# A linear-attention and two-layer float32 kernel: one elementwise line from GpSimd to ScalarE, the weight conversions' products from GpSimd to VectorE, and new instruction orders inside a step

## The chip, the cores and the metric

The kernel runs on one core of a Trainium2 chip. The metric is the device time of one execution in microseconds (us). Three executions of the kernel before took 1710.34, 1711.36 and 1712.08 us; the median is 1711.36 us. Engines are named as the profile names them: PE is TensorE's matmuls and PEld its weight loads, DVE is VectorE, ACT is ScalarE, POOL is GpSimd, SP is SyncE, which here issues the transfers.

## The reference, cut to what matters

Everything is computed to float32 precision. The weights of both layers arrive as float64; q, k and v are float32.

```python
# 8 batches, 8 heads, 576 positions, 64 per head -> x: 4608 tokens x 512
kv  = einsum('bhsd,bhse->bhde', k, v)   # k^T v per head
out = q @ kv;  x = out / sqrt(mean(out*out) + 1e-6) * g_norm
# first layer, d_ff = 2048
h = x @ w_in
P = a[0] + a[1]*h + a[2]*h*h + a[3]*h*h*h
Q = 1.0 + abs(b[0])*abs(h) + abs(b[1])*h*h
x2 = (P / (Q + 1e-6)) @ w_out
# second layer, d_ff = 1024
out = (((x2 @ w1) * (x2 @ w2)) @ w3) @ w_out2
```

## The kernel before, in words

**Number format.** A float32 operand is split into a rounded part `hi` (made by a ScalarE copy) and a rest `lo` (a VectorE or GpSimd subtraction); a product is three matmuls, hi·hi, hi·lo and lo·hi (`mm3`, L87 to L90). A float64 weight tile is turned into float32 by `to_f32` (L144): two ScalarE instructions make the sign (L149, L150), three VectorE instructions move the exponent and mantissa over (L152, L156, L160), and one product of both gives the float32 tile (L164, on GpSimd).

**Steps.** The first layer runs in 192 steps. A step g is one block of 384 tokens (12 blocks) times one slice of 128 of d_ff (16 slices). In step g TensorE computes h for that slice (`l1`, 12 matmuls of 384 columns) and then multiplies the finished activation of step g - 3 with `w_out` (`l2`, 12 matmuls). Between the two lies the elementwise work, spread over three steps:

- `ew1(g)`, in step g: ScalarE makes a = |h| (L512) and the innermost line n of the numerator P (L513). The inner line of Q, s = |b1|·a + |b0|, is L514 on GpSimd, and L517 multiplies it with a, also on GpSimd. VectorE brings the numerator further (L520, L522; both read h in PSUM).
- `ew2(g - 1)`: ScalarE makes an approximate reciprocal from s (L530, L531), VectorE improves it by a Newton step and multiplies with the numerator (L533, L535, L537). All three read two tiles of SBUF.
- `ew3(g - 2)`: ScalarE's `hi` (L502) and VectorE's `lo` (L504) of the result, which `l2` of the next step needs.

**What sets the order.** The program is scheduled by hand: each engine runs its instructions in the order in which the Python code writes them. Within a step, these pieces are generators that stop (`yield`) between VectorE instructions, and `mix` advances them by the letters of a string: n is ew1, s is ew2, l is ew3, and t, u, v are weight conversions. `MIX[0]` holds for the first 23 steps, `MIX[1]` for the others. ScalarE's and GpSimd's order follows from the same strings, since a piece's first part (up to its first `yield`) writes their instructions.

**Weight conversions.** 32 tiles of 128x512 are needed by the first layer itself: 11 are converted before step 0 and 21 in steps 0 to 22 (`CONV`). Each is also split: ScalarE copies `hi` (L84), GpSimd subtracts (L85), since `w_next` passes `nc.gpsimd` to it. 80 half tiles of 128x256 of the second layer's weights are converted from step 32 on, in 9 of 16 steps (`bg_conv`), and go back to DRAM as float32. In the last block (from step 176) the second layer's tiles are loaded again and split (`slot_split`, L625): 16 on GpSimd, 8 on VectorE.

**Attention.** The next blocks' x (36 tiles of 128 tokens) is computed between the matmuls of the steps, with small matmuls (L266, L318, L331, L373) and a few instructions each on ScalarE and VectorE. The second layer follows the steps and is TensorE's alone, apart from evictions.

Of the kernel before, what the change touches and what calls it, by code (L numbers as in the profile page):

```python
# [12 lines left out]
AF = mybir.ActivationFunctionType  # L13
# [5 lines left out]
def linear_attention_two_moe_kernel(  # L19
# [15 lines left out]
):  # L35
    """x = rmsnorm(q (k^T v)) per head; g = P(x w_in) / Q(x w_in); x2 = g w_out;
    out = ((x2 w1) * (x2 w2)) (w3 w_out2).

    The float64 weights come as their bits and become float32 on the chip (within float32's range;
    what is below it becomes 0). Float32 operands are split exactly into hi + lo float32r parts (12 + 12 bits), and a product  # L40
    is hi hi + hi lo + lo hi, accumulated in float32. Activations stay feature-major, so that the
    weights are the stationary operands as they lie in DRAM.
    """
    nc = tc.nc
# [46 lines left out]

    # ---- weights in SBUF: slot s of wa holds a [P, KD, P] slice, slot s of wb a [P, DM] row tile,
    # first as float64 bits, then as float32r hi and lo
    wa, wb = {}, {}
# [42 lines left out]
    def mix(order, **gens):  # L137
        """The generators' VectorE instructions in this order, so that none waits for the one before."""
        for c in order:
            next(gens[c], None)  # L140
        for gen in gens.values():
            run(gen)

    def to_f32(raw, t, n=W):  # L144
        """float64 bits to float32: exponent and mantissa moved over, times the sign (0 for 0 and
        for what is below float32's range). The low words' place takes the magnitude."""
        hw, lw = raw[:, :, 1], raw[:, :, 0]
        ti = t.bitcast(I32)
        nc.scalar.activation(out=ti, in_=f32(hw), func=AF.Copy, scale=0.47 * 2.0**15)  # L149
        nc.scalar.activation(out=t, in_=ti, func=AF.Sign)  # L150
        yield
        nc.vector.tensor_scalar(  # L152
            out=lw, in0=lw.bitcast(U32), scalar1=2.0**-29, scalar2=7.0, op0=ALU.mult, op1=ALU.min
        )
        yield
        nc.vector.scalar_tensor_tensor(  # L156
            out=lw, in0=hw, scalar=3, in1=lw, op0=ALU.logical_shift_left, op1=ALU.bitwise_or
        )
        yield
        nc.vector.tensor_scalar(  # L160
            out=lw, in0=lw, scalar1=0x7FFFFFFF, scalar2=0x40000000,
            op0=ALU.bitwise_and, op1=ALU.bitwise_xor,
        )
        nc.gpsimd.tensor_tensor(out=t, in0=f32(lw), in1=t, op=ALU.mult)  # L164

# [6 lines left out]
    def conv_on(depth=DEPTH):  # L172
        """The next stage of every conversion but the last depth."""
        for p in pend[:max(0, len(pend) - depth)]:
            p[1].pop(0)(p[0])
            if not p[1]:
                pend.remove(p)
# [5 lines left out]
    def conv(raw, *stages):  # L183
        """A tile's conversion; its later stages follow the starts of the next ones."""
        t = f32_tile(W)
        yield from to_f32(raw, t)
        pend.append((t, list(stages)))
        conv_on()
# [6 lines left out]

    # ---- constants
    ident = const.tile([P, P], F32, name="ident")
# [19 lines left out]

    # ---- attention
    atp_cm = tc.tile_pool(name="atp", bufs=1)
# [4 lines left out]
    def segs(i):  # L224
        """Row ranges of token tile i: (first row, rows, batch, position in the sequence)."""
        r, left = [], P
        t = i * P
        while left:
            b, s = divmod(t, S)
            n = min(left, S - s)  # L230
            r.append((P - left, n, b, s))
            t += n
            left -= n
        return r
# [20 lines left out]
    def kv_part(i, c):  # L255
        """Part c of tile i's k^T v, two heads to a product (a tile has rows of two batches at most)."""
        sg = segs(i) if i < NTILE else []
        if c >= len(sg):
            return
        kk = kt[i].rearrange("p h d -> p (h d)")  # L260
        vv = vt[i].rearrange("p h d -> p (h d)")
        r0, n, b, s = sg[c]
        if s == 0:
            kvps[0] = ps_tile("kv", [P, NP, P])
        for p in range(NP):
            nc.tensor.matmul(  # L266
                kvps[0][:, p, :],
                lhsT=kk[r0:r0 + n, p * P:(p + 1) * P],
                rhs=vv[r0:r0 + n, p * P:(p + 1) * P],
                start=(s == 0 and p == 0),  # L270
                stop=(s + n == S),
                skip_group_check=True,
            )
        if c == len(sg) - 1:
            del kt[i], vt[i]

    def kv_out(i):
        """The diagonal blocks of a batch's k^T v to SBUF, where tile i holds the batch's last row."""
        for r0, n, b, s in segs(i) if i < NTILE else []:
            if s + n == S:  # L280
                dst = kvbd[b % 2]
                nc.scalar.copy(dst[0:D, :, 0:D], kvps[0][0:D, :, 0:D])
                nc.vector.tensor_copy(dst[D:P, :, D:P], kvps[0][D:P, :, D:P])
# [10 lines left out]
    def at_tile(shape, i, name):  # L294
        """The first block's tiles have their own room, the others share one."""
        if i < T0:
            return p0[0].tile(shape, F32, tag=name, name=name)
        return atp.tile(shape, F32, tag="at", name=name)

    def at_ps(i, name):  # L300
        """The first block's tiles also have a PSUM bank each."""
        if i < T0:
            tag = {"q": ("acc0", "acc1", "acc2", "acc3"), "o": ("h", "h", "at", "acc0"), "x": ("acc1", "acc2", "acc3", "at")}[name][i]
        else:
            tag = "at"
        return ps_tile(tag, [P, NP, P], 2 if tag == "h" else 1)
# [53 lines left out]
    def n_out(i):  # L360
        """The tile times -2 / rms, by one Newton step."""
        po, ms, y, y2 = at[i]
        nc.vector.tensor_tensor(out=y2, in0=ms, in1=y2, op=ALU.mult)
        nc.vector.scalar_tensor_tensor(out=y, in0=y2, scalar=3.0, in1=y, op0=ALU.subtract, op1=ALU.mult)
        x = at_tile([P, H, D], i, "xt")
        nc.vector.tensor_tensor(out=x, in0=po, in1=y.unsqueeze(2).to_broadcast([P, H, D]), op=ALU.mult)
        at[i] = x
# [19 lines left out]
    with tc.manual_schedule():  # L387
        p0_cm = tc.tile_pool(name="p0", bufs=T0)
        p0[0] = p0_cm.__enter__()
        NKV0 = -(-S // P)  # L390
        # The steps (block, part of d_ff): the first two blocks share the first half of the weights
        # before the second half is there
        HM = MF // 2
# [17 lines left out]
        def w_next():  # L411
            kind, i = w_seq[n_cv[0]]
            n_cv[0] += 1
            return (conv_a if kind == "a" else conv_b)(i, nc.gpsimd)

# [3 lines left out]

        # What comes before the steps: loads (W weights, K k and v, Q q), C conversions, F their last stages,  # L420
        # and per token tile k k^T v, t q's transpose, o its product and squares, r rms, n normed, x split
        count = {}
# [60 lines left out]
        def x2_out(j, m):  # L483
            """The block's x2 to DRAM; the first block's comes in two parts."""
            for n in range(KD):
# [20 lines left out]
        def ew1(g):  # L506
# [6 lines left out]
            nc.scalar.activation(out=n, in_=h, func=AF.Identity, scale=na[:, 3:4], bias=na[:, 2:3])  # L513
            nc.gpsimd.tensor_scalar(  # L514
                out=s, in0=a, scalar1=ab[:, 1:2], scalar2=ab[:, 0:1], op0=ALU.mult, op1=ALU.add
            )
            nc.gpsimd.tensor_tensor(out=s, in0=s, in1=a, op=ALU.mult)  # L517
# [25 lines left out]

        # The next blocks' attention: what is done in step g at the places 0 (its start), 1 (behind the first
        # products), 2 (before the split), 3 (before the end), 4 (its end)
        todo = {}
# [40 lines left out]

        # ---- the second part's weights as float32 to DRAM, half a tile at a time
        HW = W // 2
# [26 lines left out]

        # ---- second part: out = ((x2 w1) * (x2 w2)) W
        def slot_load(kind, s, src):
# [74 lines left out]

        # ---- W = w3 w_out2: its rows take the second half of wb, w_out2 the first
        w3t = {}
# [32 lines left out]
        def w_step(i):  # L728
            """W's row i, with row i + 1's transposes; row i - 1 to SBUF."""
            if i == 0:  # L730
# [7 lines left out]

        MIX = "ttssntslntltsn", "sssnnllnnstttt"
        CONV = "11101101120111111111111"  # L740
        NG = NBA * MF
        LB = NG - MF
        for g in range(NG + SK):
            if g >= LB:
                if g > LB:
# [3 lines left out]
                    if 2 <= s and s - 2 < MF:  # L749
                        slot_split(("a", s - 2), nc.gpsimd)  # L750
                s = g - LB - SK - 1
# [92 lines left out]
```

## Time and profile before

| | us |
|---|---|
| median of three executions | 1711.36 |
| span of the profiled execution | 1712.4 |
| TensorE busy | 1615.6 (94%) |
| VectorE busy | 1134.9 (66%) |
| ScalarE busy | 831.2 (49%) |
| GpSimd busy | 612.2 (36%) |

The profile gives the span of the execution that it shows (first to last instruction), 1712.4 us, and no separate device time of that execution; the span is 1.0 us above the median of the runs. The shares of busy time mix parts of the program with different limits: before step 0, the 192 steps, and the second layer. The rows below are therefore taken from stretches of the span. Step g starts where ScalarE's L512 of that step starts: step 0 at 60.2 us, step 23 at 212.7, step 176 at 975.8, step 191 at 1045.5. Neighbouring instructions of an engine overlap a little in the trace, so what one costs its engine is the distance from its start to the next one's start.

### The profile page before, as it was taken

The numbers are of one execution on the slowest core, as the hardware profiler recorded it, in microseconds if no ns is written. First come the engines' busy times: TensorE is split into PE (matmuls) and PEld (weight loads), VectorE is DVE, ScalarE is ACT, GpSimd is POOL, SyncE is SP. The second block draws the span as 40 slices with busy tenths as digits, with TensorE's granted clock in tenths as the row PEclk, the third lists the DMA queues.
The fourth block names the chain that finished last, engine by engine and source line by source line (L and its number), as shares of the span: only waits on it lengthen the run. The fifth ranks groups of instructions, "written<-read, shape, count | busy, mean of one in ns | idle before, by whom it ended". The sixth has DMA issues, their size and how long they took to land.

```text
span 1712.4 us, 22970 instructions
## 1 busy us (share of the span) xinstructions
PE 1615.6 (94%) x8384; PEld 1450.9 (85%) x8384; DVE 1134.9 (66%) x1949; ACT 831.2 (49%) x1701; POOL 612.2 (36%) x552
## 2 busy tenths in 40 slices
PE   4777799999999999999999999999999999999999
PEld 3676799999999999999999888788888888888887
DVE  5999989999999999999999997222222222222221
ACT  4667666666666667676666675211112112111211
POOL 5689944545555555454545585000000000000000
PEclk9899999999999999999999999999999999999999
DMA  9634113333332332342212142301001001010000
GB/s 238 161 94 128 31 44 93 78 81 87 93 94 70 94 84 77 81 103 71 71 50 66 44 151 71 111 0 50 25 25 49 25 25 44 7 49 25 25 25 25
DMA packets 175154, 118.43 MB, mean 69 GB/s; under 512 B 118720, under 2 KB 152512, under 8 KB 175040
## 3 DMA queue, kind: packets, MB, share of 16 engines
q1 hardware_dynamic: 175040, 116.95, 24.7%
q8 instruction: 66, 1.08, 0.3%
q14 instruction: 48, 0.39, 0.1%
HBM read 86.77 MB, written 30.15 MB: 68 GB/s over the span
## 4 chain that ended last, share of the span: by engine, by line
PE 47%; DVE 32%; issue 7%; ACT 7%; POOL 5%; DMA 2%; SPq 1%; DVEq 0%; POOLq 0%; ACTq 0%
PE h L88 6%; PE h L90 6%; PE h L89 6%; PE acc L89 5%; PE acc L88 5%; PE acc L90 5%; DVE s L537 4%; DVE n L520 4%; DVE s L533 4%; DVE n L522 4%; DVE lo L504 4%; DVE s L535 3%; POOL s L517 2%; PE at L89 2%; PE kv L89 2%
## 5 line engine op out<-in xcount | busy, mean ns | idle before, releaser
L514 POOL TENSOR_SCALAR s<-a,ab 128x384 f32<-128x384 f32 x192 | 190.8, 994 | 198.1 <-ACT a L512 184.5
L517 POOL TENSOR_TENSOR s<-s,a 128x384 f32<-128x384 f32 x192 | 228.1, 1188 | 16.0
L530 ACT ACTIVATE y<-s,epsq 128x384 f32<-128x384 f32 x192 | 117.7, 613 | 160.7 <-POOL s L517 160.2
L535 DVE SCALAR_TENSOR_TENSOR s<-s,y 128x384 f32<-128x384 f32 x192 | 177.3, 923 | 6.0
L667 ACT COPY ab<-h 128x512 f32<-128x512 f32 x72 | 42.3, 588 | 264.7 <-PE h L90 239.0
L668 DVE TENSOR_TENSOR ab<-ab,at 128x512 f32<-128x512 f32 x36 | 24.7, 687 | 213.6 <-PE at L90 128.5
L537 DVE SCALAR_TENSOR_TENSOR s<-n,na,s 128x384 f32<-128x384 f32 x192 | 158.6, 826 | 0.0
L668 DVE TENSOR_TENSOR ab<-ab,kv 128x512 f32<-128x512 f32 x36 | 24.7, 687 | 199.7 <-PE kv L90 160.2
L504 DVE TENSOR_TENSOR lo<-s,hi 128x384 fp32r<-128x384 f32 x192 | 142.5, 742 | 0.0
L164 POOL TENSOR_TENSOR ct<-str,ct 128x256 f32<-128x256 f32 x80 | 73.0, 912 | 185.7 <-ACT hi L502 101.5
L513 ACT ACTIVATE n<-h,na 128x384 f32<-128x384 f32 x192 | 128.0, 667 | 0.0
L533 DVE SCALAR_TENSOR_TENSOR s<-s,y 128x384 f32<-128x384 f32 x192 | 111.8, 582 | 12.5 <-ACT y L531 11.9
L522 DVE SCALAR_TENSOR_TENSOR n<-n,na,h 128x384 f32<-128x384 f32 x192 | 115.4, 601 | 0.0
L520 DVE TENSOR_TENSOR n<-n,h 128x384 f32<-128x384 f32 x192 | 104.0, 542 | 1.3 <-ACT n L513 1.1
L531 ACT ACTIVATE y<-y 128x384 f32<-128x384 f32 x192 | 100.9, 526 | 6.1
L502 ACT CAST hi<-s 128x384 fp32r<-128x384 f32 x192 | 98.0, 510 | 6.6 <-DVE s L537 6.6
L512 ACT ACTIVATE a<-h 128x384 f32<-128x384 f32 x192 | 91.5, 476 | 11.2 <-PE h L90 11.2
L84 ACT CAST eh<-ab 128x512 fp32r<-128x512 f32 x36 | 22.3, 621 | 107.4 <-DVE ab L668 107.4
L84 ACT CAST el<-ab 128x512 fp32r<-128x512 f32 x36 | 22.4, 621 | 106.0 <-DVE ab L668 106.0
L266 PE MATMUL kv<-vt,kt 128*128 128x128 f32 (+1 forms) x320 | 48.3, 300 | 22.6 <-DMA vt<-in_v_dram 20.9
L266 PEld LDWEIGHTS kv<-vt,kt 128*128 128x128 f32 (+1 forms) x320 | 45.1, 210 | 25.5 <-issue 22.8
L355 ACT ACTIVATE ny<-ms 128x8 f32<-128x8 f32 x36 | 7.5, 208 | 100.4 <-DVE ms L349 100.4
(740 smaller groups left out, 5055.8 us busy)
## 6 DMA issues: line engine op xcount, KB each, us to landing
str<-in_moe_w_dram SPq DMA_DIRECT2D x64, 256.0 KB, 3.5
x2d<-xev SPq DMA_DIRECT2D x48, 192.0 KB, 3.2
x<-x2d SPq DMA_DIRECT2D x36, 256.0 KB, 3.4
out_dram<-oev SPq DMA_DIRECT2D x36, 256.0 KB, 2.2
qt<-in_q_dram SPq DMA_DIRECT2D x32, 256.0 KB, 3.2
kt<-in_k_dram SPq DMA_DIRECT2D x32, 256.0 KB, 4.2
vt<-in_v_dram SPq DMA_DIRECT2D x32, 256.0 KB, 4.5
w12d<-ct SPq DMA_DIRECT2D x32, 128.0 KB, 1.7
```

Of the source, the lines that this page charges most:

```text
L88: nc.tensor.matmul(outp, lhsT=lh, rhs=rh, start=first, stop=False)
L89: nc.tensor.matmul(outp, lhsT=lh, rhs=rl, start=False, stop=False)
L90: nc.tensor.matmul(outp, lhsT=ll, rhs=rh, start=False, stop=last)
L504: nc.vector.tensor_tensor(out=e["lo"], in0=e["s"], in1=f32(e["hi"]), op=ALU.subtract)
L513: nc.scalar.activation(out=n, in_=h, func=AF.Identity, scale=na[:, 3:4], bias=na[:, 2:3])
L514: nc.gpsimd.tensor_scalar(out=s, in0=a, scalar1=ab[:, 1:2], scalar2=ab[:, 0:1], op0=ALU.mult, op1=ALU.add)
L517: nc.gpsimd.tensor_tensor(out=s, in0=s, in1=a, op=ALU.mult)
L520: nc.vector.tensor_tensor(out=n, in0=n, in1=h, op=ALU.mult)
L522: nc.vector.scalar_tensor_tensor(out=n, in0=n, scalar=na[:, 1:2], in1=h, op0=ALU.add, op1=ALU.mult)
L533: nc.vector.scalar_tensor_tensor(out=s, in0=s, scalar=EPS_Q, in1=y, op0=ALU.add, op1=ALU.mult)
L535: nc.vector.scalar_tensor_tensor(out=s, in0=s, scalar=2.0, in1=y, op0=ALU.subtract, op1=ALU.mult)
L537: nc.vector.scalar_tensor_tensor(out=s, in0=n, scalar=na[:, 0:1], in1=s, op0=ALU.add, op1=ALU.mult)
```

## The change

1. The inner line of Q moves from GpSimd to ScalarE: L514 to L516 become one ScalarE instruction (L515 after). GpSimd keeps the product with a.
2. The last product of every conversion (`to_f32`) moves from GpSimd to VectorE, behind a `yield` of its own.
3. The subtractions of the splits that GpSimd had (`w_next`, and `slot_split` in the last block) move to VectorE.
4. Both strings of `MIX` are new. The comments and docstrings are taken out; the line numbers shift by one or so.

```diff
@@ to_f32
-        nc.gpsimd.tensor_tensor(out=t, in0=f32(lw), in1=t, op=ALU.mult)
+        yield
+        nc.vector.tensor_tensor(out=t, in0=f32(lw), in1=t, op=ALU.mult)
@@ w_next
-            return (conv_a if kind == "a" else conv_b)(i, nc.gpsimd)
+            return (conv_a if kind == "a" else conv_b)(i)
@@ ew1
-            nc.gpsimd.tensor_scalar(
-                out=s, in0=a, scalar1=ab[:, 1:2], scalar2=ab[:, 0:1], op0=ALU.mult, op1=ALU.add
-            )
+            nc.scalar.activation(out=s, in_=a, func=AF.Identity, scale=ab[:, 1:2], bias=ab[:, 0:1])
             nc.gpsimd.tensor_tensor(out=s, in0=s, in1=a, op=ALU.mult)
@@ the steps
-        MIX = "ttssntslntltsn", "sssnnllnnstttt"
+        MIX = "nlstnuntlustustut", "nlstntnltststs"
...
-                        slot_split(("a", s - 2), nc.gpsimd)
+                        slot_split(("a", s - 2), nc.vector)
```

VectorE's row of one step with a half-tile conversion, in the middle of the first layer, before:

```order
L533 SCALAR_TENSOR_TENSOR s<-s,y 128x384
L535 SCALAR_TENSOR_TENSOR s<-s,y 128x384
L520 TENSOR_TENSOR n<-n,h 128x384
L504 TENSOR_TENSOR lo<-s,hi 128x384
L522 SCALAR_TENSOR_TENSOR n<-n,na,h 128x384
L537 SCALAR_TENSOR_TENSOR s<-n,na,s 128x384
L152 TENSOR_SCALAR str<-str 128x256
L156 SCALAR_TENSOR_TENSOR str<-str 128x256
L160 TENSOR_SCALAR str<-str 128x256
```

and the same step's row after the change:

```order
L519 TENSOR_TENSOR n<-n,h 128x384
L152 TENSOR_SCALAR str<-str 128x256
L521 SCALAR_TENSOR_TENSOR n<-n,na,h 128x384
L505 TENSOR_TENSOR lo<-s,hi 128x384
L156 SCALAR_TENSOR_TENSOR str<-str 128x256
L532 SCALAR_TENSOR_TENSOR s<-s,y 128x384
L160 TENSOR_SCALAR str<-str 128x256
L534 SCALAR_TENSOR_TENSOR s<-s,y 128x384
L165 TENSOR_TENSOR ct<-str,ct 128x256
L536 SCALAR_TENSOR_TENSOR s<-n,na,s 128x384
```

The numerator's two instructions, which read h in PSUM, now come first, the three of ew2 come last, and the conversion's four (L165 is the new one) stand between them, so that none directly follows the one whose result it reads. In a step without a conversion the rows L519, L521, L505, L532, L534, L536 follow each other directly.

ScalarE's row of the same step before (from the reciprocal to the conversion's sign):

```order
L530 ACTIVATE y<-s,epsq 128x384
L531 ACTIVATE y<-y 128x384
L512 ACTIVATE a<-h 128x384
L513 ACTIVATE n<-h,na 128x384
L502 CAST hi<-s 128x384
L149 ACTIVATE ct<-str 128x256
L150 ACTIVATE ct<-ct 128x256
```

and after:

```order
L513 ACTIVATE a<-h 128x384
L514 ACTIVATE n<-h,na 128x384
L515 ACTIVATE s<-a,ab 128x384
L503 CAST hi<-s 128x384
L529 ACTIVATE y<-s,epsq 128x384
L530 ACTIVATE y<-y 128x384
L149 ACTIVATE ct<-str 128x256
L150 ACTIVATE ct<-ct 128x256
```

The reciprocal of the step before (L529, L530 after) moves from the head of the step to behind `hi`, and the new L515 stands between the numerator's line and `hi`.

VectorE's row of a step with a whole-tile conversion (steps 0 to 22), after the change; before, L165 and L85 were not on this engine:

```order
L519 TENSOR_TENSOR n<-n,h 128x384
L521 SCALAR_TENSOR_TENSOR n<-n,na,h 128x384
L152 TENSOR_SCALAR wa14r<-wa14r 128x512
L505 TENSOR_TENSOR lo<-s,hi 128x384
L532 SCALAR_TENSOR_TENSOR s<-s,y 128x384
L156 SCALAR_TENSOR_TENSOR wa14r<-wa14r 128x512
L534 SCALAR_TENSOR_TENSOR s<-s,y 128x384
L160 TENSOR_SCALAR wa14r<-wa14r 128x512
L165 TENSOR_TENSOR ct<-wa14r,ct 128x512
L85 TENSOR_TENSOR wa13hl<-ct,wa13hl 128x512
L536 SCALAR_TENSOR_TENSOR s<-n,na,s 128x384
```

The product L165 directly follows L160, whose result it reads, and the `lo` of the tile converted two conversions earlier (L85) comes right behind it. GpSimd's row is left with its set-up and 192 times L516 (the product s·a). TensorE's and SyncE's rows are the same before and after.

## Rows read from the trace of the kernel before

**Rows 1.** Busy time by stretch: us, then PE, PEld, DVE, ACT, POOL, clock, DMA, GB/s

```profile
0.00:60.20 60.20, 29.81 (x142) 26.79 (x143) 40.67 (x63) 30.89 (x57) 28.66 (x28) 0.86 1.02 237
60.20:212.70 152.50, 118.27 (x629) 108.81 (x627) 147.04 (x212) 101.12 (x195) 132.03 (x91) 0.94 0.32 90
212.70:975.80 763.10, 740.37 (x4365) 714.36 (x4366) 723.77 (x1338) 513.10 (x1113) 384.15 (x384) 1.00 0.29 77
975.80:1045.50 69.70, 66.67 (x367) 62.63 (x366) 67.54 (x105) 51.55 (x106) 61.44 (x45) 1.00 0.36 110
1045.50:1712.40 666.90, 660.51 (x2888) 538.26 (x2886) 155.88 (x234) 134.52 (x234) 5.88 (x6) 1.00 0.10 36
```

**Rows 2.** Waits, steps 23 to 175: us in total, times, longest

```profile
PEld acc L89 <- DVE lo L504: 33.8, 57, 1.4
```

**Rows 3.** Groups of VectorE, steps 23 to 175: busy us, mean ns, idle before

```profile
L535 DVE SCALAR_TENSOR_TENSOR s<-s,y 128x384 f32<-128x384 f32 x153 | 144.6, 945 | 5.3
L504 DVE TENSOR_TENSOR lo<-s,hi 128x384 fp32r<-128x384 f32 x153 | 113.4, 741 | 0.0
L537 DVE SCALAR_TENSOR_TENSOR s<-n,na,s 128x384 f32<-128x384 f32 x153 | 108.6, 710 | 0.0
L522 DVE SCALAR_TENSOR_TENSOR n<-n,na,h 128x384 f32<-128x384 f32 x153 | 92.0, 601 | 0.0
```

**Rows 4.** Timeline of VectorE, step 102 and the next one's start: start us, duration us

```profile
607.90 0.54 DVE L533 SCALAR_TENSOR_TENSOR s<-s,y 128x384 f32<-128x384 f32 x1
608.48 0.91 DVE L535 SCALAR_TENSOR_TENSOR s<-s,y 128x384 f32<-128x384 f32 x1
609.31 0.54 DVE L520 TENSOR_TENSOR n<-n,h 128x384 f32<-128x384 f32 x1
609.77 0.89 DVE L504 TENSOR_TENSOR lo<-s,hi 128x384 fp32r<-128x384 f32 x1
...
611.64 0.28 DVE L152 TENSOR_SCALAR str<-str 128x256 int32<-128x256 uint32 x1
611.96 0.43 DVE L156 SCALAR_TENSOR_TENSOR str<-str 128x256 int32<-128x256 int32 x1
612.42 0.30 DVE L160 TENSOR_SCALAR str<-str 128x256 int32<-128x256 int32 x1
612.63 0.55 DVE L533 SCALAR_TENSOR_TENSOR s<-s,y 128x384 f32<-128x384 f32 x1
```

**Rows 5.** Timeline of GpSimd, step 102

```profile
609.07 1.18 POOL L517 TENSOR_TENSOR s<-s,a 128x384 f32<-128x384 f32 x1
```

**Rows 6.** Group of GpSimd, steps 23 to 175

```profile
L517 POOL TENSOR_TENSOR s<-s,a 128x384 f32<-128x384 f32 x153 | 182.1, 1191 | 12.8
```

**Rows 7.** Timeline of TensorE, step 102

```profile
605.14 0.34 PE L88 MATMUL h<-xh,wa6hl 128*128 128x384 f32 x1
...
606.73 0.34 PE L88 MATMUL acc<-hi,wb3hl 128*128 128x384 f32 x1
...
609.08 1.58 PE L331 MATMUL at<-kvbd,qT 128*64 128x128 f32 x16
```

**Rows 8.** Groups of ScalarE, steps 23 to 175

```profile
L513 ACT ACTIVATE n<-h,na 128x384 f32<-128x384 f32 x153 | 102.0, 667 | 0.0
L530 ACT ACTIVATE y<-s,epsq 128x384 f32<-128x384 f32 x153 | 93.7, 613 | 118.8 <-POOL s L517 118.4
L531 ACT ACTIVATE y<-y 128x384 f32<-128x384 f32 x154 | 81.0, 526 | 4.9
L502 ACT CAST hi<-s 128x384 fp32r<-128x384 f32 x153 | 78.0, 510 | 0.8 <-DVE s L537 0.8
```

**Rows 9.** Groups of VectorE, steps 0 to 22

```profile
L537 DVE SCALAR_TENSOR_TENSOR s<-n,na,s 128x384 f32<-128x384 f32 x22 | 33.1, 1505 | 0.0
L535 DVE SCALAR_TENSOR_TENSOR s<-s,y 128x384 f32<-128x384 f32 x22 | 18.4, 834 | 0.1
```

**Rows 10.** Group of VectorE, whole span: a 128x512 difference of two SBUF tiles

```profile
L85 DVE TENSOR_TENSOR el<-ab,el 128x512 fp32r<-128x512 f32 x36 | 24.9, 693 | 24.7 <-ACT el L84 24.7
```

## The prediction

> **What bounds the kernel now.** I read busy time by stretch first [rows 1]. Before step 0 the transfers are busy all the time (DMA share 1.02) and VectorE only for 40.67 of 60.2 us. After step 191 TensorE alone works (660.51 of 666.9 us). Between them lie 985.3 us in which VectorE is nearly full: 147.04 of 152.5 us in steps 0 to 22, 723.77 of 763.1 in steps 23 to 175, 67.54 of 69.7 in the last block. TensorE looks as full, but its recorded matmuls overlap, so I check it by the distances of their starts: nine matmuls of 384 columns start in 1.59 us (605.14 to 606.73), 0.177 us each, and a small matmul of the attention takes 1.58 / 16 = 0.099 us [rows 7]. Steps 23 to 175 hold 153 x 24 = 3672 of the first kind and 4365 - 3672 = 693 of the second [rows 1]: 650 + 69 = 719 us of 763. TensorE therefore has 44 us to give there, at the full granted clock (1.00, the upper level of 2.4 GHz), and the waits say to whom: its longest sum is on `lo` of VectorE's L504, 33.8 us [rows 2]. So VectorE sets the pace of the steps, with TensorE 6% behind it.
>
> Next, why VectorE is so full. L533 and L535 are the same kind of instruction on the same shapes. One takes 0.54 to 0.55 us alone [rows 4], and L535 takes 0.945 in the mean [rows 3]. L522, which reads one tile of SBUF and h in PSUM, takes 0.601 in all 153 cases, while L537 of the same form with two tiles of SBUF takes 0.710. In step 102, L504 starts at 609.77 and lasts 0.89 us, while GpSimd's L517 stands from 609.07 to 610.25 [rows 4, 5]. VectorE's instructions with two SBUF inputs wait for GpSimd's. Over steps 23 to 175 that is, against 0.55 for L535 and L504 and 0.601 for L537: 0.395 + 0.191 + 0.109 = 0.695 us a step, 106.3 us in all, or 0.277 us for each us that GpSimd is busy (384.15) [rows 1, 3].
>
> The Trainium skill, SBUF — State Buffer, section Who interferes with whom, says that such a pair excludes each other and that the second to issue waits until the first has finished. By that L504 would have ended 0.55 us behind 610.25, at 610.80; it ended at 610.66, so the trace agrees but for 0.14 us. With 0.14 us more on each of 153 steps the sum below would come out 21 us higher, at 1692 us.
>
> **The change, part by part, steps 23 to 175** (763.1 us).
>
> *Taken away:* GpSimd's inner line and the conversions' products leave, and only L517 stays, 1.191 us a step [rows 6]. I first strike out all waits, -106.3 us, then put back those for the product that remains. Its price c per step has no row of its own. Below, c is 0: the product starts behind the new L515, when VectorE can be in L519 and L521, which read PSUM and do not wait. Above, it is the 1.505 - 0.601 = 0.90 us that L537 waited in steps 0 to 22 [rows 9]. By GpSimd's busy time it would be 1.191 x 0.277 = 0.33. I take 0.25, near this, and lower because the new order puts the two instructions that never wait, some 1.0 us, where the product is issued. 153 x 0.25 = +38 us, with ends at 0 and 138.
>
> *Added on VectorE:* the product L165, on 128x256 with two SBUF inputs, in 78 of these steps (80 conversions, two of them later). Its nearest row is L156, 0.43 us [rows 4]. What it costs depends on the order. An instruction behind an independent one starts about 0.08 before that one's end (L520 lasts 0.54, L504 starts 0.46 behind it), while behind the one whose result it reads it starts 0.58 after a start of 0.54 [rows 4]: 0.12 us of difference. The old chain L152, L156, L160 takes 0.32 + 0.46 + 0.21 = 0.99 [rows 4]. The new four, each less 0.08, take 0.20 + 0.35 + 0.22 + 0.35 = 1.12. That is +0.13, and the old pair L533, L535 no longer stands together in these steps, -0.12: about +1 us for 78. In the other 75 steps nothing separates L519 from L521 or the three of ew2: three dependent pairs in place of one, +0.24 x 75 = +18 us.
>
> *Moved on ScalarE:* the reciprocal now stands behind `hi`, and `hi` needs the last instruction of VectorE's previous step. From there ScalarE needs 0.510 + 0.613 + 0.526 = 1.65 us [rows 8] until VectorE's L532 can start. VectorE covers it with L519, L521 and L505, 0.58 + 0.52 (its 0.60 less 0.08) + 0.46 = 1.56, and in steps with a conversion with two more. I take 0.12 us of waiting for the 75 others, +9 us; 0 below (attention work stands between in many), 0.3 above. The new L515 itself is like L513, 0.667 us [rows 8]; its cover is that ScalarE works only 513.10 of 763.1 us [rows 1]. With 153 x 0.667 more it is at 615, or 81%. Queued behind L515 on ScalarE are `hi` and the reciprocal, priced just now. The wait of ScalarE for GpSimd before the reciprocal (118.4 us [rows 8]) goes, since the product has most of a step to finish.
>
> Sum: 763.1 - 106.3 + 38 + 1 + 18 + 9 = 723 us, **-40 us**. TensorE's 719 lie just below: it is what is late next, and stops the gain at 44.
>
> **The other stretches.** *Steps 0 to 22:* 21 conversions put a product and a subtraction on VectorE, each like the 128x512 difference of 0.693 us [rows 10] less 0.08 of overlap: 21 x 1.22 = +25.6. Order: +2. Waits struck out: L537 22 x 0.904 = 19.9 and L535 22 x 0.284 = 6.2 [rows 9]; L504 and the conversion's own instructions stand in the same queue without a row here, between 0 and as much again, taken at half, 13. One product remains per step, here in a longer row of instructions with two SBUF inputs: 0.5 x 23 = +11.5 (ends 0.25 and 0.90). Net about 0, between -12 and +15. *Last block:* GpSimd's 61.44 us [rows 1] x 0.277 = -17; 16 subtractions x 0.61 = +10; 15 steps x (0.25 + 0.24) = +7. Net 0, give or take 5. *Before step 0:* 11 products and as many subtractions, 13 us of VectorE work in a stretch with 19.5 us to spare and GpSimd's waits gone: 0, give or take 3. *After step 191:* nothing moves, 0. The order of SyncE's transfers stays; a half tile's store now waits for VectorE's product in place of GpSimd's, with nobody behind it in haste.
>
> Altogether -40 us on a span of 1712.4, which is 1.0 above the median of the runs; on the median, 1711.4 - 40 = **1671 us**.
>
> **The rivals.**
> - *ScalarE's row becomes the one that is late.* Nine instructions of it run in one order, and VectorE might wait for the reciprocal in all 153 steps by 0.25 us, not in 75 by 0.12: 38 - 9 = +29 us, 1700 us. For it: `hi`, the reciprocal and the sign now follow one another behind L515. Against it: two or three instructions more cover this in 78 steps.
> - *Slower: the product that remains stands ahead of `lo`.* If ScalarE runs in step with VectorE, L515 ends when VectorE is done with L521, the product starts, and L505 and TensorE's `l2` behind it wait. At c = 0.90 this is 153 x 0.65 = +100 us, 1771 us. It decides from c = 0.25 + 40 / 153 = 0.51 on. For it: L537 waits 0.90 in steps 0 to 22 [rows 9], with more than one GpSimd instruction in a row. Against it: in steps without a conversion only 2.2 of some 4.7 us can wait.
> - *No change.* The Trainium skill, Perfetto Trace Analysis, section Optimizing Scalar/DVE Operations, warns that shifting work between GpSimd and VectorE may not help since they share a read port. As a mechanism here: what VectorE no longer waits, it now works, or c comes out at 0.5; 1708 to 1714 us. Against it: L164's place on VectorE costs next to nothing in the sum above, because it fills a gap in a dependent chain.
>
> **How the numbers follow.** The forecast, with TensorE just below VectorE, holds 1656 to 1688: the low end has c at 0 (44 us), and 11 us from the first steps and the rest; the high end has c at 0.36. Chance 0.65. ScalarE late, 1688 to 1704: 0.20. No change: 0.05. Slower: 0.10. The range 1656 to 1704 holds the first two less the tails, about 0.8. A measurement of this kernel can tell about 0.2% (3.4 us) from no change. Faster 0.85, same 0.05, slower 0.10.
>
> **What would show it.** Right: in steps 23 to 175 L534 and L505 fall to 0.55 to 0.65 us in the mean, GpSimd is busy some 182 us there, a block of 16 steps takes near 75.6 us (80 before), and TensorE's wait for `lo` shrinks. Wrong: L505, L532 or L536 stay at 0.8 us or more (the product stands ahead of them), L532 waits for ScalarE's reciprocal by more than 10 us in all (ScalarE), or steps 0 to 22 take over 168 us.

## The result, and the profile after

The changed kernel takes 1684.14 us (median of four executions, 1683.86 to 1684.72) against 1711.72 for the kernel before: a ratio of 0.9841, interval 0.9827 to 0.9855. It is faster by 27.6 us, where 40 were forecast. The span of the profiled execution falls by 29.9 us, from 1712.4 to 1682.5; the sums below go by spans. The execution of the kernel before that was profiled was some 2.5 us slower than its median (in the other runs the time lies 1.8 us above the profiled span), so the spans show a little too much.

Where they went is read from busy time by stretch, in the columns of [rows 1]. The steps are cut at the same places as there: before step 0, steps 0 to 22, steps 23 to 175, the last block, the rest.

```profile
0.00:62.20 62.20, 31.24 (x142) 28.02 (x143) 39.52 (x81) 29.65 (x56) 1.63 (x8) 0.84 0.97 227
62.20:207.30 145.10, 116.44 (x623) 108.24 (x623) 139.40 (x254) 113.06 (x219) 26.36 (x23) 0.94 0.33 95
207.30:947.60 740.30, 729.34 (x4369) 715.07 (x4368) 678.58 (x1420) 600.44 (x1265) 158.53 (x153) 1.00 0.30 79
947.60:1018.80 71.20, 65.90 (x370) 63.51 (x369) 69.06 (x118) 61.18 (x120) 16.66 (x15) 1.00 0.33 108
1018.80:1682.50 663.70, 658.62 (x2888) 537.22 (x2886) 157.64 (x239) 136.16 (x238) 1.03 (x1) 1.00 0.10 36
```

| stretch | before | after | difference | forecast |
|---|---|---|---|---|
| before step 0 | 60.2 | 62.2 | +2.0 | 0 |
| steps 0 to 22 | 152.5 | 145.1 | -7.4 | 0 (-12 to +15) |
| steps 23 to 175 | 763.1 | 740.3 | -22.8 | -40 |
| last block | 69.7 | 71.2 | +1.5 | 0 (-5 to +5) |
| after step 191 | 666.9 | 663.7 | -3.2 | 0 |

In steps 23 to 175 VectorE now has 62 us without work (39 before), TensorE has 11 by its row (23 before), and GpSimd has 158.53 us of work instead of 384.15. VectorE's groups there, in the columns of [rows 3]:

```profile
L505 DVE TENSOR_TENSOR lo<-s,hi 128x384 fp32r<-128x384 f32 x153 | 113.2, 740 | 0.0
L521 DVE SCALAR_TENSOR_TENSOR n<-n,na,h 128x384 f32<-128x384 f32 x153 | 93.2, 609 | 2.6
L536 DVE SCALAR_TENSOR_TENSOR s<-n,na,s 128x384 f32<-128x384 f32 x152 | 93.1, 613 | 2.6
L532 DVE SCALAR_TENSOR_TENSOR s<-s,y 128x384 f32<-128x384 f32 x153 | 84.4, 552 | 6.1 <-ACT y L530 1.7
L534 DVE SCALAR_TENSOR_TENSOR s<-s,y 128x384 f32<-128x384 f32 x152 | 83.9, 552 | 2.6
L519 DVE TENSOR_TENSOR n<-n,h 128x384 f32<-128x384 f32 x153 | 83.7, 547 | 28.1 <-ACT n L514 27.6
L152 DVE TENSOR_SCALAR str<-str 128x256 int32<-128x256 uint32 x79 | 33.6, 425 | 0.0
...
L165 DVE TENSOR_TENSOR ct<-str,ct 128x256 f32<-128x256 f32 x78 | 32.2, 413 | 0.0
```

Of the three that waited for GpSimd before, L535 and L537 (now L534 and L536) are down at about their lengths alone, 0.552 and 0.613 us. `lo` (L505) is where it was, 0.740 in place of 0.741 [rows 3]. The new idle time is in front of L519, the first instruction that reads h: 28.1 us, nearly all for ScalarE's L514. The waits of the same steps (us in total, times, longest) say what ScalarE waited for:

```profile
ACT a L513 <- PE h L90: 57.0, 66, 2.5
DVE n L519 <- ACT n L514: 27.6, 38, 1.5
...
PEld acc L89 <- DVE lo L505: 3.9, 5, 0.8
...
DVE s L532 <- ACT y L530: 1.7, 9, 0.5
```

TensorE's wait for `lo` has shrunk from 33.8 us [rows 2] to 3.9. In its place ScalarE waits for TensorE's h, and VectorE for ScalarE. Before the change VectorE hardly stood there:

```profile
DVE s L533 <- ACT y L531: 7.2, 20, 1.3
...
DVE n L520 <- ACT n L513: 1.1, 4, 0.3
```

One step shows both readings. VectorE's timeline (start, duration, in brackets the wait before):

```profile
596.00 0.60 DVE L536 SCALAR_TENSOR_TENSOR s<-n,na,s 128x384 f32<-128x384 f32 x1
598.12 0.56 DVE L519 TENSOR_TENSOR n<-n,h 128x384 f32<-128x384 f32 x1 [1.52 <-ACT n L514]
598.72 0.61 DVE L521 SCALAR_TENSOR_TENSOR n<-n,na,h 128x384 f32<-128x384 f32 x1
599.25 0.95 DVE L505 TENSOR_TENSOR lo<-s,hi 128x384 fp32r<-128x384 f32 x1
600.27 0.56 DVE L532 SCALAR_TENSOR_TENSOR s<-s,y 128x384 f32<-128x384 f32 x1
```

and GpSimd's:

```profile
598.76 1.02 POOL L516 TENSOR_TENSOR s<-s,a 128x384 f32<-128x384 f32 x1 [4.91 <-ACT s L515]
```

VectorE stood 1.52 us for L514, which needs h. ScalarE's timeline says what this time went to:

```profile
597.04 0.49 ACT L513 ACTIVATE a<-h 128x384 f32<-128x384 f32 x1 [1.54 <-PE h L90]
597.42 0.67 ACT L514 ACTIVATE n<-h,na 128x384 f32<-128x384 f32 x1
```

ScalarE too had stood for h. From h's arrival at 597.04 its L513 and L514 took until 598.09, 1.05 us, and VectorE stood for these as well. Of the 38 waits of L519, 37 follow an L513 that had itself waited for h; by the timelines some 26 of their 27.6 us fall into such 1.05 us behind h. Below, "VectorE's wait for h" means both together. An order with L514 ahead of L513 was not tried.

L521, with h in PSUM, ran beside the product; L505, with two tiles of SBUF, took 0.40 us longer than its 0.55. The product ended at 599.78. By the rule of the Trainium skill, SBUF — State Buffer, section Who interferes with whom, L505 would then have ended at 600.33; it ended at 600.20, 0.13 us earlier, the same small difference as before the change.

### The profile page after: what moved, and what is told of

Same layout as the page of the kernel before. It is cut to its first block, busy times and chain, and to the rows that moved or that the text cites. A ratio compares the mean times of both kernels' runs of the same rounds, so it can differ in the third digit from the quotient of the medians.

```text
span 1682.5 us, 22953 instructions
## 1 busy us (share of the span) xinstructions
PE 1601.5 (95%) x8384; PEld 1452.1 (86%) x8384; DVE 1084.2 (64%) x2109; ACT 940.5 (56%) x1893; POOL 204.2 (12%) x200
## 4 chain that ended last, share of the span: by engine, by line
PE 52%; DVE 28%; issue 5%; ACT 5%; DMA 1%; SPq 0%; DVEq 0%
PE h L88 7%; PE h L90 7%; PE h L89 7%; PE acc L89 6%; PE acc L90 6%; PE acc L88 6%; DVE s L536 4%; DVE lo L505 4%; DVE s L532 4%; DVE s L534 3%; DVE n L519 3%; PE kv L89 2%; PE at L89 2%; PE kv L88 2%; PE at L88 2%
## 5 line engine op out<-in xcount | busy, mean ns | idle before, releaser
L516 POOL TENSOR_TENSOR s<-s,a 128x384 f32<-128x384 f32 x192 | 202.6, 1055 | 816.7 <-ACT s L515 816.7
L505 DVE TENSOR_TENSOR lo<-s,hi 128x384 fp32r<-128x384 f32 x192 | 135.9, 708 | 0.0
L515 ACT ACTIVATE s<-a,ab 128x384 f32<-128x384 f32 x192 | 135.5, 706 | 0.0
L536 DVE SCALAR_TENSOR_TENSOR s<-n,na,s 128x384 f32<-128x384 f32 x192 | 130.1, 678 | 3.3
L513 ACT ACTIVATE a<-h 128x384 f32<-128x384 f32 x192 | 93.5, 487 | 63.2 <-PE h L90 62.9
L514 ACT ACTIVATE n<-h,na 128x384 f32<-128x384 f32 x192 | 128.2, 667 | 0.0
L519 DVE TENSOR_TENSOR n<-n,h 128x384 f32<-128x384 f32 x192 | 104.9, 546 | 29.6 <-ACT n L514 29.2
L521 DVE SCALAR_TENSOR_TENSOR n<-n,na,h 128x384 f32<-128x384 f32 x192 | 117.2, 610 | 4.0
L529 ACT ACTIVATE y<-s,epsq 128x384 f32<-128x384 f32 x192 | 118.7, 618 | 0.0
L532 DVE SCALAR_TENSOR_TENSOR s<-s,y 128x384 f32<-128x384 f32 x192 | 105.9, 552 | 7.1 <-ACT y L530 2.5
L534 DVE SCALAR_TENSOR_TENSOR s<-s,y 128x384 f32<-128x384 f32 x192 | 106.1, 552 | 3.2
L530 ACT ACTIVATE y<-y 128x384 f32<-128x384 f32 x192 | 101.0, 526 | 6.1
L150 ACT ACTIVATE ct<-ct 128x256 f32<-128x256 int32 (+1 forms) x112 | 53.7, 480 | 3.5
L356 ACT ACTIVATE ny<-ms 128x8 f32<-128x8 f32 x36 | 7.5, 209 | 77.4 <-DVE ms L350 77.4
```

The costliest lines, as they stand in the source:

```text
L505: nc.vector.tensor_tensor(out=e["lo"], in0=e["s"], in1=f32(e["hi"]), op=ALU.subtract)
L515: nc.scalar.activation(out=s, in_=a, func=AF.Identity, scale=ab[:, 1:2], bias=ab[:, 0:1])
L519: nc.vector.tensor_tensor(out=n, in0=n, in1=h, op=ALU.mult)
L529: nc.scalar.activation(out=y, in_=s, func=AF.Abs_reciprocal_sqrt, bias=epsq[:, 0:1])
L532: nc.vector.scalar_tensor_tensor(out=s, in0=s, scalar=EPS_Q, in1=y, op0=ALU.add, op1=ALU.mult)
L534: nc.vector.scalar_tensor_tensor(out=s, in0=s, scalar=2.0, in1=y, op0=ALU.subtract, op1=ALU.mult)
```

## The experiments

The changes to the code are given against the changed kernel unless it says otherwise. Ratios are to the kernel before, on the same chip.

| run | us | ratio, interval | steps 0–22 | steps 23–175 | last block |
|---|---|---|---|---|---|
| before | 1711.72 | 1 | 152.5 | 763.1 | 69.7 |
| the change | 1684.14 | 0.9841 (0.9827–0.9855) | 145.1 | 740.3 | 71.2 |
| p1 products back | 1695.96 | 0.9912 (0.9897–0.9927) | 143.7 | 747.7 | 79.0 |
| p2 line back | 1689.35 | 0.9876 (0.9860–0.9891) | 141.2 | 745.6 | 76.4 |
| p3 old orders | 1727.86 | 1.0097 (1.0078–1.0115) | 139.7 | 790.2 | 71.3 |
| p4 new orders alone | 1704.28 | 0.9957 (0.9940–0.9974) | 151.1 | 747.3 | 80.3 |
| c0 no product | 1662.52 | 0.9714 (0.9698–0.9730) | 136.2 | 733.2 | 65.8 |
| t1 11 matmuls | 1674.97 | 0.9783 (0.9768–0.9797) | 144.9 | 731.0 | 72.0 |
| t2 before, 11 matmuls | 1708.02 | 0.9978 (0.9968–0.9987) | 152.5 | 761.2 | 69.4 |
| t3 c0 and t1 | 1642.85 | 0.9596 (0.9582–0.9610) | 136.3 | 715.1 | 65.4 |
| m1 old first order | 1678.22 | 0.9804 (0.9789–0.9818) | 138.6 | 741.6 | 71.1 |
| q1 later turn of q | 1767.63 | 1.0326 (1.0309–1.0343) | 145.1 | 823.2 | 71.2 |
| e1 later splits | 1683.64 | 0.9833 (0.9818–0.9847) | 145.1 | 740.5 | 69.1 |
| m1, q1 and e1 | 1760.12 | 1.0284 (1.0267–1.0301) | 138.6 | 821.3 | 69.1 |

The stretches are those of one execution, the profiled one; in p2 and p3 it took 4.0 and 3.5 us more than the median.

**Which part pays: parts undone one by one.** The theory was that of the prediction: fewer GpSimd instructions, fewer waits.

p1, the conversions' products and the splits back on GpSimd:

```diff
-        yield
-        nc.vector.tensor_tensor(out=t, in0=f32(lw), in1=t, op=ALU.mult)
+        nc.gpsimd.tensor_tensor(out=t, in0=f32(lw), in1=t, op=ALU.mult)
...
+            return (conv_a if kind == "a" else conv_b)(i, nc.gpsimd)
...
+                        slot_split(("a", s - 2), nc.gpsimd)
```

> The change without its parts 2 and 3: the conversions' products and the splits' subtractions are on GpSimd again, the inner line of Q stays on ScalarE, the new orders stay. Theory (what pays is that VectorE waits for fewer GpSimd instructions, one priced at about 0.25 us of waiting): in steps 23 to 175 VectorE saves 78 x 0.36 us of work and waits 78 x 0.25 us more, about -9 us there; in steps 0 to 22 GpSimd has 21 x 3.1 us more, VectorE 21 x 1.22 less to do and about 0.277 x 66 = 18 more to wait, about -8 to +3; last block 16 subtractions back, -5 to +3. Together 1670 to 1692 us, so the products' move is worth nothing or costs. Rival (the products' move is what pays): 1700 us or more.

p2, Q's inner line back on GpSimd:

```diff
-            nc.scalar.activation(out=s, in_=a, func=AF.Identity, scale=ab[:, 1:2], bias=ab[:, 0:1])
+            nc.gpsimd.tensor_scalar(
+                out=s, in0=a, scalar1=ab[:, 1:2], scalar2=ab[:, 0:1], op0=ALU.mult, op1=ALU.add
+            )
```

> The change without its part 1: the inner line of Q is on GpSimd again, in front of the product, all else as in the change. Theory: 0.86 us more of GpSimd in each of 192 steps, at 0.277 us of waiting per us of GpSimd, is 0.24 us a step or 46 us, part of it under TensorE's pace: 1710 to 1735 us, no faster than the kernel before, and VectorE's instructions with two SBUF inputs are long again. Rival (the new orders carry the gain): 1684 to 1695 us.

p3, both old orders with the new engines:

```diff
-        MIX = "nlstnuntlustustut", "nlstntnltststs"
+        MIX = "ttssntslntltsn", "sssnnllnnstttt"
```

> The change with the two strings of before, so the same instructions on the same engines in the old order. Theory: the waits for one GpSimd product a step stay at 0.2 to 0.4 us wherever it falls, and a chain of four dependent conversion instructions costs 0.3 us in 78 steps, 1684 to 1705 us. Rival (the new orders carry the gain, by placing the product beside the two instructions that read PSUM): 1708 us or more.

p4, the kernel before with the new orders (the same edit of MIX in the other direction):

> The kernel before with the two new strings alone. Theory: GpSimd keeps all its instructions, so VectorE's waits stay near 0.7 us a step: 1700 to 1725 us. Rival (the new orders carry the gain): 1695 us or less.

p1 gave 1696, between the two ranges; p2 1689, in the rival's; p3 1728, 16 us slower than before; p4 1704, in the theory's. The theory falls all the same. With the new orders, steps 23 to 175 take 740 to 748 us with GpSimd at 158 us of work there (the change), 230 (p1), 299 (p2) or 360 (p4). With the old orders and 165 us of it they take 790. The rows of p1, p2, p4 and p3:

```profile
203.20:950.90 747.70, 731.75 (x4362) 717.31 (x4363) 688.75 (x1340) 600.99 (x1265) 229.61 (x234) 1.00 0.30 79
```

```profile
203.10:948.70 745.60, 730.11 (x4367) 714.34 (x4365) 682.04 (x1420) 517.92 (x1112) 298.96 (x306) 1.00 0.30 79
```

```profile
210.80:958.10 747.30, 732.05 (x4362) 715.36 (x4362) 692.34 (x1340) 518.02 (x1112) 359.78 (x387) 1.00 0.30 79
```

```profile
202.00:992.20 790.20, 742.66 (x4362) 714.11 (x4363) 736.54 (x1417) 607.65 (x1266) 165.09 (x153) 1.00 0.28 74
```

The times alone could hide a price, since TensorE's 719 us lie just under 740. VectorE's busy time, which holds its waits for GpSimd, does not. The change, p2 and p3 give VectorE the same instructions: it is busy 678.58 us in the change, 682.04 in p2 with 140 us more of GpSimd's work, and 736.54 in p3 with 7 us more of it. The new orders alone (p4) take VectorE's busy time from 723.77 to 692.34.

The groups of VectorE and one wait of TensorE in p3, same steps:

```profile
L505 DVE TENSOR_TENSOR lo<-s,hi 128x384 fp32r<-128x384 f32 x153 | 116.4, 761 | 12.0 <-ACT hi L503 11.5 <-PE acc L90 0.4
L532 DVE SCALAR_TENSOR_TENSOR s<-s,y 128x384 f32<-128x384 f32 x153 | 111.4, 728 | 1.6 <-ACT y L530 1.0
L534 DVE SCALAR_TENSOR_TENSOR s<-s,y 128x384 f32<-128x384 f32 x153 | 99.9, 653 | 5.3
```

```profile
PEld acc L89 <- DVE lo L505: 54.6, 64, 1.3
```

On these three lines one product a step then costs 0.21 + 0.18 + 0.10 = 0.49 us against 0.55 alone, 75 us in all where the change has 40, and TensorE waits for `lo` longer than before. One step of p3 shows the place, VectorE's rows and GpSimd's:

```profile
610.38 0.55 DVE L519 TENSOR_TENSOR n<-n,h 128x384 f32<-128x384 f32 x1
610.85 1.04 DVE L505 TENSOR_TENSOR lo<-s,hi 128x384 fp32r<-128x384 f32 x1
```

```profile
610.47 1.00 POOL L516 TENSOR_TENSOR s<-s,a 128x384 f32<-128x384 f32 x1 [4.06 <-ACT s L515]
```

In the old row only L519, which reads h in PSUM, stands between the ew2 lines and `lo`; in the new row L519 and L521 both stand ahead of `lo`. So a us of GpSimd's work has no price of its own: what stands in VectorE's row when it is issued sets it. That the orders make the difference is shown by the runs; that it is by these places is read from the rows of single steps. The price is not all of p3's loss either. Against the kernel before its steps take 27 us more: VectorE is busy 13 us more, with L165 now in its row, and stands 11.5 us before L505 for ScalarE's `hi`, where it stood for nothing before [rows 3].

The parts lean on each other. The new orders alone give 7 us; the new engines under the old orders lose 16; both together give 28. The line's move (p2) is worth 5 of these and the products' and splits' (p1) 12: 7.8 in the last block (79.0 to 71.2) and 7.4 in steps 23 to 175, less some 4 that p1 is faster before step 23. In the last block the new orders alone lose 10.6 us (69.7 to 80.3), which was not looked into. The Trainium skill, Perfetto Trace Analysis, section Optimizing Scalar/DVE Operations, warns that shifts between GpSimd and VectorE may not help. Under the old orders p3 agrees, though it also moves a line to ScalarE: 16 us slower. Under the new ones it did not hold: p1, without that shift, is 11.8 us slower than the change.

**What ends the gain at 740.** In the changed kernel two things might: the price of the product that is left, or TensorE. c0 leaves the product out (Q is then |b1|·|h| + |b0| alone); t1 leaves out one of the twelve matmuls of h; t2 is the same cut in the kernel before; t3 is c0 and t1 together.

```diff
-            nc.gpsimd.tensor_tensor(out=s, in0=s, in1=a, op=ALU.mult)
```

> The change without the last GpSimd product s = s a, which is left out (Q becomes |b0| + |b1| |h|), so VectorE never waits for GpSimd in the steps. In the changed kernel L505 waits 0.19 us in each of 153 steps (steps 23 to 175) and L152 0.14 in 79, 40 us in all. Theory (in the new order TensorE's h paces these steps: L519 waits 28 us for it, in each of the four kernels with the new order that ran so far): the 40 us turn into longer waits of L519, and the stretch of 740 us falls by only 5 to 18 us; 1662 to 1679 us in all. Rival (VectorE's work still sets the pace): 30 to 40 us less there, 1640 to 1655 us.

```diff
-                mm3(h, wh[:, c, :], wl[:, c, :], xh[:, c, :], xl[:, c, :], c == 0, c == KD - 1)
+                if c:
+                    mm3(h, wh[:, c, :], wl[:, c, :], xh[:, c, :], xl[:, c, :], False, c == KD - 1)
+                else:
+                    nc.tensor.matmul(h, lhsT=wh[:, c, :], rhs=xh[:, c, :], start=True, stop=False)
+                    nc.tensor.matmul(h, lhsT=wl[:, c, :], rhs=xh[:, c, :], start=False, stop=False)
```

> The change with 11 in place of 12 matmuls in l1 (the product of hi with lo of the first 128 features is left out): TensorE has 0.174 us a step less, 27 us in steps 23 to 175. Theory (TensorE paces them now): 15 to 27 us less in that stretch. Rival (VectorE still paces): 0 to 8 us less.

> The kernel before with the same 11 matmuls in l1. Theory (VectorE paces the kernel before, TensorE waits for its lo): 0 to 8 us less in steps 23 to 175. Rival (TensorE paced both kernels): 15 to 27 us less.

> The change without the last GpSimd product and with 11 matmuls in l1 (the two cuts of c0_no_product and t1_after_cut together; both parts of the computation are left out). Alone they gave 7 and 9 us of the 740 in steps 23 to 175, out of 40 us of VectorE's waits and 27 us of matmuls. Theory (TensorE and VectorE take turns in setting the pace, step by step, so what one gains is lost in the steps in which the other is late): together they give clearly more than 16, 24 to 36 us in that stretch. Rival (a third thing paces the steps, ScalarE's row or the chain through one step): 16 us or less.

Steps 23 to 175: c0 -7.1 us, t1 -9.3, t2 -1.9 (against the kernel before), t3 -25.2. The kernel before had room on TensorE, as forecast: 27 us less of matmuls (153 x 0.177) gave it 1.9. In the changed kernel neither cut alone gives its full worth, 40 us of VectorE's waits or 27 of matmuls, and the two together give 25.2 where their sum is 16.4. So c0, t2 and t3 came out as their theories had it, and t1 between its two. (c0's whole gain is 21.6 us: 8.9 lie in steps 0 to 22 and 5.4 in the last block.) The busy rows of c0, t1 and t3:

```profile
198.00:931.20 733.20, 726.29 (x4362) 716.51 (x4363) 642.18 (x1420) 599.08 (x1265) 0.00 (x0) 1.00 0.30 80
```

```profile
205.20:936.20 731.00, 712.37 (x4215) 688.47 (x4214) 679.70 (x1419) 598.33 (x1265) 157.94 (x153) 1.00 0.30 80
```

```profile
197.40:912.50 715.10, 702.49 (x4213) 688.85 (x4212) 639.42 (x1419) 597.01 (x1265) 0.00 (x0) 1.00 0.31 82
```

Two groups of VectorE and two of its waits in c0:

```profile
L505 DVE TENSOR_TENSOR lo<-s,hi 128x384 fp32r<-128x384 f32 x153 | 84.2, 551 | 0.0
...
L152 DVE TENSOR_SCALAR str<-str 128x256 int32<-128x256 uint32 x79 | 22.8, 289 | 0.0
```

```profile
DVE n L518 <- ACT n L514: 44.5, 53, 1.8
DVE s L531 <- ACT y L529: 16.5, 45, 0.4
```

Without the product L505 and L152 are at their lengths alone, so the 40 us are gone from there. They come back as waiting: VectorE's wait for h rises from 27.6 us to 44.5, and its wait for ScalarE's reciprocal from 1.7 to 16.5. These 16.9 and 14.8 with the 7.1 gained are 38.8 of the 40. In t1 the wait for h falls to 17.5, and TensorE stands longer for VectorE, for `lo` 14.0 us instead of 3.9 and before L319 14.2 instead of 9.7:

```profile
DVE n L523 <- ACT n L518: 17.5, 26, 2.3
PEld at L319 <- DVE xl L383: 14.2, 17, 1.1
PEld acc L89 <- DVE lo L509: 14.0, 36, 1.0
```

So the two engines take turns in setting the pace, with ScalarE's row between them: where VectorE is ahead, it is h and what ScalarE does with it that come late, and where TensorE is ahead, VectorE's results. Four of six neighbouring steps of the changed kernel, in the columns of [rows 1]:

```profile
597.04:603.26 6.22, 6.22 (x38) 6.22 (x37) 4.54 (x8) 3.41 (x8) 1.02 (x1) 1.00 0.21 59
...
610.98:615.91 4.93, 4.85 (x30) 4.53 (x29) 4.86 (x12) 4.31 (x10) 1.01 (x1) 1.00 0.51 115
615.91:621.04 5.13, 5.13 (x34) 5.13 (x33) 5.13 (x13) 4.34 (x10) 1.09 (x1) 1.00 0.46 128
621.04:627.27 6.23, 6.23 (x38) 6.23 (x37) 4.99 (x9) 3.41 (x9) 1.02 (x1) 1.00 0.22 66
```

TensorE's matmuls fill all four, or nearly (4.85 of 4.93 us). The steps of 4.93 and 5.13 us hold 12 and 13 instructions of VectorE (a conversion), which fill them as well. In those of 6.22 and 6.23 VectorE has 8 and 9 and over 1 us to spare. So these steps show TensorE setting the pace, alone or with VectorE; that VectorE sets it in others rests on c0 and t1. These two are not long by TensorE's work for one step: 38 recorded matmuls are more than a step's 24 large ones, since TensorE went on into the next step's. What put off the L513 that ends them is ScalarE's own row, in which L356 of the attention stands ahead of it and waits for VectorE's L350:

```profile
626.91 0.21 ACT L356 ACTIVATE ny<-ms 128x8 f32<-128x8 f32 x1 [2.75 <-DVE ms L350]
```

In the 16 steps looked at, the change has three of 6.2 us and one of 5.9, and their sum is 77.31 us, 80.39 before.

**Versions that might beat it.** m1 puts the first string of MIX back (steps 0 to 22) and keeps the new second one. q1 turns q one step later, with the aim of spreading TensorE's work of a long step. e1 puts the last block's splits behind a step's elementwise work.

```diff
+        MIX = "ttssntslntltsn", "nlstntnltststs"
```

> The change with the old string for steps 0 to 22 and the new one for the others. In the change those 23 steps take 145.0 us, in the change with both old strings 139.7. Theory (the strings act on their own stretches, and the first new one costs 5 us): 1676 to 1681 us. Rival (the first string only shifts work into the later steps): 1683 to 1686 us.

```diff
-                when = ((q_pe, 0, 4), (q_next, 0, 4), (q_out, 1, 0), (o_pe, 1, 4), (n_sq, 2, 0), (n_rms, 2, 2),
+                when = ((q_pe, 1, 1), (q_next, 1, 1), (q_out, 1, 2), (o_pe, 1, 4), (n_sq, 2, 0), (n_rms, 2, 2),
```

> The change with q's transposes (L319) of the blocks from the fourth on behind the next step's first products instead of at their own step's end, with the copy of their result behind that step's elementwise work. In the change TensorE stands 5 to 7 us in steps 23 to 175 before L319, for VectorE's L383. Theory (turns): TensorE's stop goes and L519's waits for h shrink by as much, 3 to 10 us faster than the change, 1674 to 1681 us. Rival (TensorE's stops are slack): 1683 to 1686 us.

```diff
-                        slot_split(("a", s - 2), nc.vector)
...
-                    slot_split(("b", s - 2), nc.vector)
...
+            if g > LB and 0 <= g - LB - 3 < MF:
+                slot_split(("a", g - LB - 3), nc.vector)
+            if g >= LB and 0 <= g - LB - SK - 3 < KF2:
+                slot_split(("b", g - LB - SK - 3), nc.vector)
```

> The change with the last block's splits (L627) behind a step's elementwise work instead of ahead of it. In the change the steps with two splits take 5.7 to 5.9 us every other time, since VectorE's two subtractions at the head of its row wait for ScalarE's two copies. Theory (that wait is what is late there): the last block falls from 71.2 to 64 to 69 us, 1677 to 1682 us in all. Rival (VectorE's work itself): 70 us or more, 1683 to 1686 us.

> The change with the old first string (m1_old_first), q's transposes later (q1_later_turn) and the late splits (e1_late_splits). If the three act on their own stretches: 1678 us less what the other two give, 1668 to 1676 us. If only the old first string counts: 1678 us.

m1 came out at 1678.22 us as expected, 5.9 under the change and 33 under the kernel before: the best of the versions that leave nothing out. Its gain lies in steps 0 to 22. L536 there, in the change and then in m1 (1505 ns before, as L537 [rows 9]):

```profile
L536 DVE SCALAR_TENSOR_TENSOR s<-n,na,s 128x384 f32<-128x384 f32 x22 | 23.3, 1060 | 0.1
```

```profile
L536 DVE SCALAR_TENSOR_TENSOR s<-n,na,s 128x384 f32<-128x384 f32 x22 | 16.4, 743 | 0.0
```

That is 22 x 0.317 = 7.0 us of waiting gone from L536, and the steps are 6.5 shorter. Why the old string places the product better there was not tried further.

q1 was expected to gain and lost 83 us; both theories on it were wrong. Its waits, steps 23 to 175:

```profile
DVE n L519 <- ACT n L514: 108.8, 37, 4.9
...
PEld at L332 <- ACT qT L324: 68.7, 27, 2.9
```

Turned later, q's copy by ScalarE (L324) comes to stand behind that step's elementwise row, and TensorE, in its own order, waits for it at L332, some 2.5 us in each of 27 tiles. VectorE's wait for h rises from 27.6 us to 108.8. Those 68.7 us are most of the loss. e1 took 2.1 us from the last block (71.2 to 69.1, just short of its theory's 64 to 69) and left the total within what can be told apart. With all three edits, each stretch is near that of the kernel that had its edit alone, and the total (1760 us) misses its forecast by what q1 lost.

## Why the prediction was right or wrong

**The sign and the range were right; the gain came out a third smaller than forecast.** Point by point, steps 23 to 175:

- *The waits struck out, and c = 0.25 for the product that is left.* Right in size. L505 is 0.19 us over 0.55 in 153 steps (29.1 us), and L152, the first of a conversion, 0.425 in place of the 0.282 that it had before, in 79 (11.3 us): 40 us, or 0.26 a step. Both waits are gone in c0. The sign named for it was half wrong: L534 fell to 0.55 to 0.65 as said, L505 did not, since the product still runs when it is issued. GpSimd is busy 158.5 us and not 182, as the product takes 1.036 us in place of 1.191 [rows 6].
- *The product L165 and the dependent neighbours.* L165 takes 0.413 (0.43 forecast). L521 starts 0.60 us behind L519's start in the step shown, for 0.58 forecast.
- *VectorE's wait for the reciprocal, 9 us more.* It is 1.7 us, where the kernel before had 7.2: 5.5 less. ScalarE's new row, 600.44 us of 740.3, held VectorE up for the reciprocal in 9 steps and not in all; that rival did not come. It comes in c0, with 16.5 us in 45 steps.
- ***The step that failed: "TensorE's 719 lie just below: it is what is late next, and stops the gain at 44."*** The time was taken as the larger of two sums, VectorE's 723 and TensorE's 719. VectorE's own part came out near its sum: without its waits for h and the reciprocal it fell by 43.8 us, from 763.1 - 7.2 - 1.1 = 754.8 to 740.3 - 27.6 - 1.7 = 711.0, where 106.3 - 38 - 1 - 18 = 49.3 stood. But with two sums so close each engine is the later one in some steps, and what the other has left over there is not kept. VectorE's wait for h had no term in the sum: it rose from 1.1 us to 27.6. These 26.5 and the 5.5 of its own part, less the 14.5 by which the reciprocal came out better than its +9, are the 17 us between 723 and 740. That both hold the pace is shown by c0, t1 and t3: 7.1 and 9.3 us alone, 25.2 together.
- *The other stretches.* Steps 0 to 22 gained 7.4 where 0 stood, inside the ends given. The last block's +1.5 and the +2.0 before step 0 are inside theirs. The 3.2 us after step 191, where nothing moves, are not the change's: t2, which has the code of the kernel before there, took 663.0 us for that stretch, where the profiled execution of the kernel before took 666.9.

**The rivals.** "The product stands ahead of `lo`" is what happens in place in many steps but not in price: c is 0.26, and it was to decide from 0.51 on. p3 is near that rival: 0.49 us on L505, L532 and L534, with L165 at 0.480 for 0.413 and L160 at 0.394 for 0.283 on top in the steps with a conversion, and the steps 27 us slower than before. So the condition was the right one, and the new orders are what kept the change on its good side. The sum of the prediction did not see that: it struck the waits out with the instructions that left GpSimd, while p4 gets 16 of the 23 us with those instructions still there. "No change" did not come: VectorE's busy time fell by 45 us.

**The chances.** Faster by over 0.2% at 0.85 came true. The time lies in the part of the range that the forecast itself had, 1656 to 1688, near its high end. That end was given to c = 0.36; c was 0.26, and the wait for h is what brought it there. That it is in this part is luck: without the 7.4 us of steps 0 to 22, whose terms had summed to 0, it would be at 1691.5, in the range but in the part given to a late ScalarE.

## What to carry to other kernels

When two engines' sums over a stretch lie within a few per cent of each other, as here, do not take the larger for the time: look at single steps, see which engine fills which, and cut each alone and both together to learn how much is lost in turns. What VectorE waits for GpSimd was set here by what stands in VectorE's row when GpSimd's instruction is issued, not by GpSimd's busy time; try the instructions that read PSUM there. Before a producer is moved later in an engine's row, list who waits for it in order on the next engine, as q1 shows.

## What the runs showed of the hardware

- L152, a TENSOR_SCALAR with a single SBUF input of 128x256, was not thought to wait for GpSimd. Its mean rose from 0.282 to 0.425 us when it came to stand where the product is issued. It is the product: in c0, which leaves only that out, the mean is 0.289.
- The product's own mean length on GpSimd depends on the order too: 1.191 us before, 1.046 with the new orders alone (p4), 1.036 in the change.
- In q1 and in the version with all three edits, with TensorE standing for q's copy, the granted clock over steps 23 to 175 was 0.97 in the mean, where the other kernels had 1.00 (the upper level, 2.4 GHz).
- Left open: how much of the 29 us of waiting a deeper look-ahead between h and VectorE would give back (more tiles for h were not tried), and the places of the conversions in the 16 steps.
